# Output rows of a fused attention, MoE and MLP kernel: one transfer per sequence instead of one per block

## The chip, the cores and the metric

One core of a Trainium2 chip runs the whole kernel as one program. The metric is the device time of an execution in microseconds; a table below gives it for the kernel before. TensorE (PE in the profile) does the matrix products, VectorE (DVE) and ScalarE (ACT) the elementwise work, GpSimd (POOL) a few copies and the gathers, and SyncE (SP) does nothing but issue transfers. ScalarE can issue transfers too, on a queue of its own.

## The reference

Three stages, the output of one being the input of the next:

```python
attn_out = _attn_ref(q, k, v, i_gate, f_gate, o_gate)   # (2, 8, 768, 40), a recurrence over 768 steps
x = attn_out.transpose(0, 2, 1, 3).reshape(1536, 320)    # rows: sequence b = 0, then sequence b = 1
x = _moe_ref(x, w_gate, w_noise, noise, w1, w2)          # top 2 of 8 experts, 320 -> 1024 -> 320, relu
h = x @ w_in                                             # 320 -> 2048
g = h * np.clip(h + 3.0, 0.0, 6.0) / 6.0
return g @ w_out                                         # (1536, 320) float32
```

Rows 0 to 767 of the output belong to the first sequence, rows 768 to 1535 to the second.

## The kernel before

The 1536 rows are handled in 12 blocks of 128. Attention works on 64 time steps of both sequences at once, so a block k holds, in partitions 0 to 63, steps 64k to 64k+63 of sequence 0, and in partitions 64 to 127 the same steps of sequence 1. This layout stays through all three stages. The list `rows` (line 231) names the two halves of the partitions: `rows[0]` is 0 to 63 and `rows[1]` is 64 to 127.

The schedule is written out by hand. After the attention, a list of units is worked off in order: nine of the experts, then six of the last MLP. Each unit of the MLP holds four blocks, 512 rows in all, and one half `g` of the 2048 hidden features; three units do the first half, three the second. Of a unit, `L1` (a first product, an activation on ScalarE and VectorE that ends in a tile `hb`) and `L2` (the second product, accumulated in four PSUM banks `u.acc`, one for each block) alternate over eight slices of features. `hbs` holds the `hb` tiles whose `L2` is still to be issued, and `drain` issues them and calls `finish` at the last one of a unit.

`finish(u, tiles)` (line 893) takes the finished banks out. For an expert it copies them to a tile `yo` and sends that to the DRAM tensor `Yd` (line 919), with 128 rows or, for the last tile of a full expert, 64. For the first three MLP units it leaves a sixth of the sums in SBUF (`part`). For the last three, on which the change bears, VectorE adds bank and `part` into a `yo` tile of 128 x 320 fp32 (line 921; four buffers), and SyncE sends that tile to the output (line 923):

```python
outr = out.rearrange("(b k t) d -> k b t d", b=B, k=NT)          # line 889
V.scalar_tensor_tensor(y, u.acc[i][:, 0:DM], 1.0 / 6.0, part, OP.mult, OP.add)
nc.sync.dma_start(outr[k], y)                                    # line 923
```

`outr[k]` is a view of 2 x 64 x 320: two stretches of the output, each 64 rows of 1280 bytes that lie one behind another, and 768 rows apart. So there are 12 output transfers of 160 KB: four behind the unit before the last but one, four behind the last but one, and four at the very end. The last unit is cut differently from the others. With `v` and `w` the two last `hb` tiles, the kernel ends like this (lines 1226 to 1232):

```python
v, w = hbs
L2(*v, (0, 1, 2))
L2(*w, (0, 1))
finish(units[-1], (0, 1))
L2(*v, (3,))
L2(*w, (2, 3))
finish(units[-1], (2, 3))
```

Nothing is computed after the second `finish`; the program ends when its last transfer has landed. Line 1294 closes the program, and waits for all transfers are put down to it.

Of the kernel before, what the change touches and what calls it, by code (L numbers as in the profile page):

```python
# [23 lines left out]
B, H, S, D = 2, 8, 768, 40  # L24
# [44 lines left out]
def mlstm_moe_mlp(ctx, tc, qk, kv, on, gf, gf6, wg, nz, w1, w2, w_in, w_out, cf, cb, cs, ci, out):  # L69
    nc = tc.nc  # L70
    V, A, G, T = nc.vector, nc.scalar, nc.gpsimd, nc.tensor
# [159 lines left out]
    rows = [slice(0, 64), slice(64, 128)]  # L231
# [500 lines left out]
    def unit(e, tiles, nf=8):  # L732
        u = U()
        u.e, u.tiles, u.nf = e, tiles, nf
        u.N = sum(n for _, n in tiles)
        u.off, o = [], 0
        for _, n in tiles:
            u.off.append(o)
            o += n
        u.half = u.N - 64 if tiles[-1][1] == 64 else None  # L740
        u.bg = {}
        u.xo = 0
        u.st = e % 2
        u.l1 = [0, 1, 7]
        return u
# [4 lines left out]
    units = [unit(0, first), unit(1, first2), unit(1, rest2)]  # L750
# [138 lines left out]
    outr = out.rearrange("(b k t) d -> k b t d", b=B, k=NT)  # L889
# [3 lines left out]
    def finish(u, tiles=None):  # L893
        for i, (s, n) in enumerate(u.tiles):
            if tiles and i not in tiles:
                continue
            if u.e >= 8:
                if not parts:
                    parts.append(wp.tile([128, 5120], F32, name="SA1"))
                part = parts[0][:, s // 128 * DM:(s // 128 + 1) * DM]  # L900
            if u.e >= 8 and u.g == 0:

                if i % 2:
                    V.tensor_scalar(part, u.acc[i][:, 0:DM], 1.0 / 6.0, None, OP.mult)
                else:
                    A.mul(part, u.acc[i][:, 0:DM], 1.0 / 6.0)
                continue
            y = wp.tile([128, DM], F32, name="yo", bufs=4)
            if u.e < 8:
                if n == 64:  # L910
                    y2 = wp.tile([64, DM], F32, name="yo2", bufs=1)
                    A.copy(y2, u.acc[i][64:128, 0:DM])
                    V.tensor_tensor(y[0:64], u.acc[i][0:64, 0:DM], y2, OP.add)
                elif i % 2:
                    V.tensor_copy(y, u.acc[i][:, 0:DM])
                else:
                    A.copy(y, u.acc[i][:, 0:DM])
                r = OV + (7 - u.e) * CAP + s
                nc.sync.dma_start(Yd[r:r + n], y[0:n])
            else:  # L920
                V.scalar_tensor_tensor(y, u.acc[i][:, 0:DM], 1.0 / 6.0, part, OP.mult, OP.add)  # L921
                k = s // 128
                nc.sync.dma_start(outr[k], y)

    zy = []

# [195 lines left out]
    def drain(k):  # L1122
        while len(hbs) > k:
            v = hbs.pop(0)
            L2(*v)
            spot[0] += 1
            u, f, lo, hi = v[0:4]
            if f == u.nf - 1 and u.i == M0:
                finish(u, range(lo, hi))
            elif u.steps[-1] == v[1:4]:  # L1130
                finish(u)
# [95 lines left out]
# [5 lines that stand above are left out]
# [66 lines left out]
```

## Time and profile before

| what | us |
|---|---|
| three runs | 574.27, 573.12, 571.0 |
| their median | 573.12 |
| the profiled execution, its own time | 572.06 |
| its span, first to last instruction | 570.3 |
| outside the span in that execution | 1.76 |
| mean granted clock of TensorE, share of full | 0.913 |

The page of the profile gives each engine's busy time, then the span in 40 equal slices of 14.3 us: a digit is the busy share in tenths, and the lowest lines give the share of the 16 DMA engines that was busy and the bytes that they moved. Other views list a stretch's instructions in order of time, cut a stretch into windows, name the chain of work that ended last, and say who waited for whom. "SPq" and "ACTq" are the sequencers of SyncE and ScalarE, on which transfers are issued. A transfer's issue is one instruction there; the bytes move later and show only in the DMA columns.

### The profile page before, as it was taken

Reading aid. Unit: us, or ns where it says so; the run is one execution under the profiler, and the core shown is the slowest. Engines: PE = TensorE matmul, PEld = TensorE weight load, DVE = VectorE, ACT = ScalarE, POOL = GpSimd, SP = SyncE. Lnnn points to the kernel's source line nnn. Section 1 sums busy time; section 2 is a strip of 40 time slices with the busy share of each in tenths; the row PEclk is TensorE's granted clock in tenths of the full one; section 3 lists DMA queues with packets and bytes.
Section 4 is the critical chain, followed back from the end, with each engine's and each line's share of the span. In section 5 each row is a group of like instructions: output and inputs, shape, how many; then the busy total and the mean of one; then the engine's idle time right before and its main releaser. Section 6 shows DMA issues by size and latency. Waiting matters only on the chain. (4 is left out here: it accounts for less than half of the span.)

```text
span 570.3 us, 10786 instructions
## 1 busy us (share of the span) xinstructions
PE 511.8 (90%) x4154; PEld 454.1 (80%) x4159; DVE 345.5 (61%) x841; ACT 227.5 (40%) x469; POOL 130.8 (23%) x164
## 2 busy tenths in 40 slices
PE   4768897786799999999999999998999999999990
PEld 1446675565689999999999899988989999999980
DVE  5167856474576587878787877467696434343440
ACT  4142433213345453545444453354553333333320
POOL 4133253534731320201111002548300100000000
PEclk9795757677879999999999999999999999999996
DMA  7697879502548478788878769678633400010101
GB/s 233 160 245 229 212 92 95 101 30 63 136 121 270 166 259 281 277 278 280 265 280 282 246 236 297 191 226 278 165 112 115 139 1 0 1 35 12 35 16 43
DMA packets 46846, 92.74 MB, mean 163 GB/s; under 512 B 7128, under 2 KB 30520, under 8 KB 46792
## 3 DMA queue, kind: packets, MB, share of 16 engines
q1 hardware_dynamic: 38980, 69.29, 41.8%
q0 software_dynamic: 6464, 19.94, 11.6%
q10 hardware_dynamic: 1348, 2.79, 1.6%
q8 instruction: 33, 0.54, 0.4%
q14 instruction: 21, 0.17, 0.1%
HBM read 68.73 MB, written 23.07 MB: 161 GB/s over the span
## 5 line engine op out<-in xcount | busy, mean ns | idle before, releaser
L861 DVE SCALAR_TENSOR_TENSOR r<-r,bank 128x512 f32<-128x512 f32 (+1 forms) x56 | 34.2, 610 | 83.2 <-ACT r L860 81.5
L846 PE MATMUL bank<-XH,SB 128*128 128x448 f32 (+3 forms) x280 | 78.9, 352 | 0.5 <-PEq L944 0.3
L849 ACT ACTIVATE hb<-bank 128x448 fp32r<-128x448 f32 (+2 forms) x80 | 37.2, 468 | 96.8 <-PE bank L846 75.2
L860 ACT ACTIVATE r<-bank,cft 128x512 f32<-128x512 f32 (+1 forms) x56 | 35.0, 626 | 98.5 <-PE bank L846 88.8
L846 PE MATMUL bank<-XL,SB 128*128 128x448 f32 (+3 forms) x192 | 68.9, 359 | 0.0
L882 PE MATMUL bank<-SB,hb 128*128 128x320 f32 x192 | 62.0, 323 | 3.3 <-ACT hb L833 3.3
L773 POOL DMA_INDIRECT XG<-Xd,idx x32 | 32.4, 1011 | 134.6 <-PE bank L783 106.7
L882 PE MATMUL bank<-SA,hb 128*128 128x320 f32 x192 | 61.0, 318 | 0.9 <-issue 0.9
L883 PE MATMUL bank<-SA,hb 128*128 128x320 f32 x192 | 59.7, 311 | 0.3 <-issue 0.3
L884 PE MATMUL bank<-SA,hb 128*128 128x320 f32 x192 | 59.7, 311 | 0.1
L884 PE MATMUL bank<-SB,hb 128*128 128x320 f32 x192 | 59.7, 311 | 0.0
L883 PE MATMUL bank<-SB,hb 128*128 128x320 f32 x192 | 59.2, 309 | 0.0
L846 PEld LDWEIGHTS bank<-XH,SB 128*128 128x128 f32 x280 | 51.5, 193 | 5.8 <-issue 1.2
L846 PE MATMUL bank<-XH,SA 128*128 128x448 f32 (+2 forms) x200 | 53.1, 337 | 2.3 <-issue 2.3
L882 PEld LDWEIGHTS bank<-SB,hb 128*128 128x128 f32 x192 | 36.2, 188 | 5.0 <-ACT hb L833 3.9
L846 PE MATMUL bank<-XL,SA 128*128 128x448 f32 (+2 forms) x120 | 40.1, 335 | 0.0
L846 PEld LDWEIGHTS bank<-XL,SB 128*128 128x128 f32 x192 | 36.8, 192 | 3.0 <-DVE XL L785 0.2
L846 PEld LDWEIGHTS bank<-XH,SA 128*128 128x128 f32 x200 | 36.1, 193 | 3.7 <-issue 1.7
L242 PE MATMUL bank<-qk 128*64 128x128 f32 x192 | 23.1, 375 | 17.3 <-DMA qk<-in_qk_dram 11.3
L883 PEld LDWEIGHTS bank<-SA,hb 128*128 128x128 f32 x192 | 36.4, 189 | 2.2 <-issue 1.1
L882 PEld LDWEIGHTS bank<-SA,hb 128*128 128x128 f32 x192 | 36.4, 190 | 1.7 <-issue 0.5
L855 DVE SCALAR_TENSOR_TENSOR hb<-bank,hb 128x64 fp32r<-128x64 f32 x64 | 14.1, 221 | 38.5 <-ACT hb L849 37.1
(198 smaller groups left out, 1152.8 us busy)
## 6 DMA issues: line engine op xcount, KB each, us to landing
raw<-in_w_dram SPq DMA_DIRECT2D x18, 640.0 KB
raw<-in_w_dram SPq DMA_DIRECT2D x18, 512.0 KB
qk<-in_qk_dram SPq DMA_DIRECT2D x22, 240.0 KB
craw<-in_w_in_dram SPq DMA_DIRECT2D x8, 640.0 KB
craw<-in_w_out_dram SPq DMA_DIRECT2D x8, 640.0 KB
raw<-in_w_dram SPq DMA_DIRECT2D x18, 256.0 KB
Yd<-yo SPq DMA_DIRECT2D x24, 160.0 KB
kv<-in_kv_dram SPq DMA_DIRECT2D x11, 324.0 KB
```

What stands on the lines that cost most here:

```text
L242: T.matmul(s4[rows[b], 2 * p:2 * p + 2, :], q[:, p, 1, rows[b]], q[:, p, 0:4:3, rows[b]], start=True, stop=True)
L773: G.indirect_dma_start(out=XG[0:n, (u.xo + i) % 4, :], out_offset=None, in_=Xd[0:CUT[u.i] * 128] if early else Xd[:, :], in_offset=bass.In ...
L846: T.matmul(p, a, b, start=(i == 0), stop=(i == 7))
L849: A.activation(hb[:, 0:N], p, AF.Relu)
L855: V.scalar_tensor_tensor(hb[:, N:N + 64], p[:, o:N], 0.0, hb[:, o:N], OP.max, OP.subtract)
L860: A.activation(r, p, AF.Relu, bias=three)
L861: V.scalar_tensor_tensor(r, r, 6.0, p, OP.min, OP.mult)
L882: T.matmul(p, h, wh, start=s, stop=False)
L883: T.matmul(p, h, wl, start=False, stop=False)
L884: T.matmul(p, hb[:, lo:lo + 128], wh, start=False, stop=t)
```

## The change

Each output block is sent as two transfers of 64 rows, one for each sequence, from the two halves of the partitions. For the first eight blocks both go out on SyncE's queue. For the four blocks of the last unit the first sequence's half goes out on SyncE's queue, the second's on ScalarE's.

```diff
@@ -920,7 +920,9 @@
             else:
                 V.scalar_tensor_tensor(y, u.acc[i][:, 0:DM], 1.0 / 6.0, part, OP.mult, OP.add)
                 k = s // 128
-                nc.sync.dma_start(outr[k], y)
+
+                for b in range(B):
+                    (A if b and u is units[-1] else nc.sync).dma_start(outr[k, b], y[rows[b]])
```

## Rows read from the trace of the kernel before

**Rows 1.** The page: busy share, transfers and bytes in 40 slices.

```profile
span 570.3 us, 10786 instructions
PE 511.8 (90%) x4154; PEld 454.1 (80%) x4159; DVE 345.5 (61%) x841; ACT 227.5 (40%) x469; POOL 130.8 (23%) x164
PE   4768897786799999999999999998999999999990
DMA  7697879502548478788878769678633400010101
```

**Rows 2.** The chain of waits from 553.5 us: start, length, what; its end.

```profile
554.55 0.16 PE bank L884
554.71 0.02 issue
554.73 0.49 DVE yo L921
```

**Rows 3.** Windows over the end: engines' busy us, clock, DMA share, GB/s.

```profile
554.50:555.50 1.00, 0.19 (x2) 0.00 (x0) 0.72 (x2) 0.00 (x0) 0.00 (x0) 1.00 0.13 35
557.50:562.50 5.00, 0.00 (x0) 0.00 (x0) 0.00 (x0) 0.00 (x0) 0.00 (x0) 0.68 0.13 49
562.50:567.50 5.00, 0.00 (x0) 0.00 (x0) 0.00 (x0) 0.00 (x0) 0.00 (x0) 0.50 0.13 49
568.80:568.90 0.10, 0.00 (x0) 0.00 (x0) 0.00 (x0) 0.00 (x0) 0.00 (x0) 0.50 0.05 13
569.00:570.30 1.30, 0.00 (x0) 0.00 (x0) 0.00 (x0) 0.00 (x0) 0.00 (x0) 0.50 0.00 0
```

**Rows 4.** Waits of SyncE's sequencer after 552 us: total us, times, longest.

```profile
SPq L1294 <- DMA out_dram<-yo: 9.0, 3, 3.3
```

**Rows 5.** Transfers after 553 us: packets by size, and the issues.

```profile
DMA packets 521, 0.66 MB, mean 38 GB/s; under 512 B 8, under 2 KB 520, under 8 KB 520
out_dram<-yo SPq DMA_DIRECT2D x4, 160.0 KB
```

**Rows 6.** VectorE in order of time, 552.5 to 556 us, waits in brackets.

```profile
552.97 0.93 DVE L921 SCALAR_TENSOR_TENSOR yo<-bank,SA 128x320 f32<-128x320 f32 x2 [1.05 <-PE bank L884]
554.29 0.93 DVE L921 SCALAR_TENSOR_TENSOR yo<-bank,SA 128x320 f32<-128x320 f32 x2 [0.39 <-PE bank L884]
```

**Rows 7.** Line 923 on SyncE: first issue, third issue, then durations in ns.

```profile
553.49 0.51 SPq L923 DMA_DIRECT2D out_dram<-yo  x1
554.81 1.45 SPq L923 DMA_DIRECT2D out_dram<-yo  x1
...
L923 SPq DMA_DIRECT2D out_dram<-yo x12: 511/908/3523, 501.1 to 556.4; - x12
```

**Rows 8.** A 64-row transfer of line 919: issue, then windows of its bytes.

```profile
358.96 0.49 SPq L919 DMA_DIRECT2D Yd<-yo  x1
...
360.00:360.10 0.10, 0.10 (x2) 0.10 (x2) 0.00 (x0) 0.10 (x1) 0.00 (x0) 1.00 0.00 0
360.20:360.30 0.10, 0.10 (x3) 0.10 (x2) 0.09 (x1) 0.00 (x0) 0.00 (x0) 1.00 0.88 205
360.30:360.40 0.10, 0.10 (x2) 0.10 (x2) 0.10 (x1) 0.00 (x0) 0.00 (x0) 1.00 0.93 205
360.50:360.60 0.10, 0.10 (x3) 0.10 (x2) 0.10 (x1) 0.00 (x0) 0.00 (x0) 1.00 0.22 52
360.60:360.70 0.10, 0.10 (x3) 0.10 (x3) 0.03 (x1) 0.00 (x0) 0.00 (x0) 1.00 0.01 0
```

**Rows 9.** Both queues' issues at the start; then ScalarE's last instruction.

```profile
0.73 1.88 ACTq L101 DMA_DIRECT2D ont<-in_on_dram  x4
...
0.74 0.42 SPq L87 DMA_DIRECT2D gft<-in_gf_dram  x1
1.22 0.40 SPq L89 DMA_DIRECT2D cbt<-in_cb_dram  x1
...
550.58 0.62 ACT L833 CAST hb<-r 128x512 fp32r<-128x512 f32 x1 [0.24 <-DVE r L861]
```

**Rows 10.** The first four output blocks: a window, and line 921's waits.

```profile
505.00:510.00 5.00, 5.00 (x30) 4.55 (x29) 1.29 (x2) 1.75 (x3) 0.00 (x0) 1.00 0.13 49
...
DVE yo L921 <- PE bank L884: 1.4, 2, 1.1
```

## The prediction

> **What bounds the kernel now.** I read the page first. TensorE is busy for 90% of the span and at nine tenths or more in nearly every slice of the second half, so this is a kernel bound by matrix products, but its last slice shows a 0 [rows 1]. The reader should stop there: a slice is 14.3 us long, and in that one the busiest engine does nothing while the DMA line still shows a 1. Next I read the chain of waits at its end. It runs along TensorE's second product and stops with VectorE's addition into `yo`, which starts at 554.73 us and takes 0.49 [rows 2]. The span is 570.3 us [rows 1], so 15.1 us lie behind the end of the chain, which follows instructions and not the bytes of a transfer.
>
> The windows show what fills them. From 554.5 us on the DMA engines move 35 and then a steady 49 GB/s, at a busy share of 0.13 of 16 engines; the last bytes move in the window from 568.8 to 568.9, and after that nothing moves until the end of the span [rows 3]. 0.13 of 16 is 2.1: two engines carry all of it. The stretch holds four transfers of 160 KB, 0.66 MB in 512 packets of 1280 bytes and 8 small ones [rows 5]. SyncE's closing waits say the same in another way: it waits three times for these transfers, 9.0 us in all, 3.3 at the longest [rows 4]. So the four blocks land one behind another, some 3.3 us apart. That is 128 rows on two engines: at 49 GB/s for both, one engine moves 1280 bytes in 1280/24.5 = 52 ns, and 64 x 52 ns = 3.34 us. The view of the output that is sent has an outermost count of two (the sequences), each a stretch of 64 rows; two engines with 64 packets each fits that.
>
> **The change part by part.** *Four blocks at the end, two transfers of 64 rows each.* The trace has no 64-row output transfer, but it has one of the very same shape: an expert's last tile goes to `Yd` as 64 rows of 1280 bytes from 64 partitions to consecutive rows. The one at 358.96 us ran when nothing else moved: issued for 0.49 us, no bytes up to 360.1, then 0.88 and 0.93 of the 16 engines busy at 205 GB/s, and done at 360.6 [rows 8]. So that transfer is spread over about all 16 engines and its last byte moves 1.64 us after its issue began. There are eight such transfers in the trace; this is the one with a quiet surrounding. I take it for the price of a half block, since it differs from the halves in the change only in the tensor written and, for every second one, in the partitions read (64 to 127).
>
> *When the last one is issued.* The additions of the four blocks come in pairs, 552.97 to 553.90 and 554.29 to 555.22 [rows 6], and their times don't hang on the transfers, since the four `yo` buffers were free: line 921 waited for TensorE alone [rows 10]. The first issue now starts at 553.49, right behind the first addition [rows 7], so it stays. On SyncE four issues of 64 rows remain. The third block's starts at 554.81 as now [rows 7]; at 0.49 us [rows 8] it ends at 555.30. Between two issues of SyncE lie 0.06 us at the start of the kernel (0.74 + 0.42 to 1.22) [rows 9]; with a wait to pass I estimate 0.1. So the fourth starts at 555.4, a little after its data are there at 555.22. In the old kernel the third issue took 1.45 and others up to 3.52 us [rows 7]; I read this as the issue being held up behind transfers that don't drain, which goes away with them, and nobody waits for it either way except the next issue.
>
> *ScalarE's queue.* Its four issues run beside SyncE's. ScalarE's last instruction of work ends at 551.2 us [rows 9], so nothing is queued behind the waits for VectorE that the new issues bring: the cover is complete, and were there still an activation to come it would have waited till 555.2. Whether two queues can issue side by side the start of the kernel shows: four issues on ScalarE fill 0.73 to 2.61 us while SyncE issues at 0.74 and 1.22 for 0.42 and 0.40 us each [rows 9]. At 0.47 us per issue the fourth half of ScalarE starts at 555.25 to 555.4 too. Both last transfers together are 160 KB; beside each other on 16 engines at the 205 GB/s of one or more they can delay each other by at most the 0.5 us that one moves bytes [rows 8], which goes into the range.
>
> *The end.* From the last byte (568.9) to the end of the span lie 1.4 us without a byte [rows 3]: landing, SyncE's last waits, the close. I keep them. SyncE's other closing waits, which now fall into the shadow of the transfers, then run from 555.9 on, while the last half is under way, so they cost nothing.
>
> *Eight earlier blocks.* Their transfers ran at the same 0.13 and 49 GB/s, but with TensorE busy 5.00 of 5.00 us beside them [rows 10], and no one waits for them. Eight more issues on SyncE, 4 us, lie in stretches where it waits for VectorE. Nothing gained, nothing lost. Two transfers that read one tile may give VectorE one more wait per `yo` buffer in the last unit; below 0.1 us, by the 0.02 us "issue" piece of the chain [rows 2].
>
> *The sum.* 555.4 + 1.64 + 1.4 = 558.45 us of span, against 570.3: 11.8 us less. On the profiled execution's own time that is 572.06 - 11.8 = 560.3 us. That execution lies 1.06 us below the median of the runs (573.12), from which it would be 561.3. All four known executions have a mean of 572.6, and I take 572.6 - 11.8 = 560.8 us.
>
> *Bounds.* Most favourable: both last halves are issued the moment VectorE is done, 555.22, and the issue costs as little as the 0.40 us of the row at 1.22 [rows 9]: 555.22 + 1.55 + 1.4 = 558.2, 12.1 less. Least favourable with the spread intact: the eight issues go one by one, 0.6 us apart, as if there were one queue. Then the last starts at 553.49 + 7 x 0.6 = 557.7 and the span is 560.7, 9.6 less; spreading over eight engines instead of 16 (512 packets / 8 x 52 ns = 3.3 us from 554.6 on, end at 559.4) lies between. Against the runs shown: 571.0 - 12.1 = 558.9 and 574.27 - 9.6 = 564.7.
>
> [...]
>
> **The rivals.** *No gain.* The halves go one after another at the present pace, two engines for each: 8 x 32 x 52 ns = 13.3 us, as now, and 572.6 us. For it speaks that block transfers to this very tensor have never run faster than 49 GB/s in the trace [rows 3, 10]; against it the 64-row transfer at 205 GB/s with the same inner stretch [rows 8]. Chance 4%. [...]
>
> *Slower.* Today each sequence's stretch of 64 rows sits on one engine. If the spread were made by that stretch, so that a transfer of one stretch goes whole to one engine, and to the same one each time, all eight halves would queue there: 512 x 52 ns = 26.6 us instead of 13.3, so 572.6 + 13.3 = 585.9 us. It decides by the number of engines of a half: with two it is a draw, with one the change loses, with more it wins. Rows 8 speak against it, as a single engine can't be 0.93 of 16. Chance 3%.
>
> *Issue-bound.* The spread works but issuing on the two queues goes in file, or the first transfer on ScalarE's queue after more than 540 us starts late; 9.6 us gained, 563.0 us. The rows at the start speak against it [rows 9], but no row shows ScalarE issuing late in the kernel. Chance 9%.
>
> **How the numbers follow.** Forecast 84%, issue-bound 9%, no gain 4%, slower 3%. The first two lie in 558.9 to 564.7, so the range is that; leaving out the other two costs under 1 in 10. A measurement of this kernel can tell about 0.5%, 2.9 us, from no change; both cases of a gain are far beyond it. Faster 0.93, same 0.04, slower 0.03.
>
> **What would show it.** In the profile after: the windows behind the last addition show a DMA share well above 0.13, in peaks toward 0.9, and GB/s in the hundreds; the last byte moves near 557.0 us; SyncE's closing wait for the output shrinks from three waits and 9.0 us to about one of 1.5; line 923 has 20 issues on SyncE and 4 on ScalarE of about 0.5 us, none over 1; the span is near 558.5, its part up to 555.2 as before. A share that stays at 0.13 or falls to 0.06 would show the prediction wrong (no gain, slower), and a last issue past 556 us would point to the issue-bound case.

## The result, and the profile after

| | before | after |
|---|---|---|
| median, us | 572.67 (4 runs) | 557.51 (4 runs) |
| lowest to highest, us | 571.0 to 574.27 | 556.19 to 567.38 |
| profiled execution: time, span, us | 572.06, 570.3 | 556.19, 554.4 |
| ratio after/before, 95% interval | | 0.9728 [0.9681, 0.9775] |

One of the four executions after, at 567.38 us, ran in a slower state (mean granted clock of TensorE 0.899, where the other three have 0.916 to 0.932), and the ratio leaves it out.

The kernel became faster by 15.2 us in the medians, 15.9 in the two profiled executions. Forecast were 11.8 us and 560.8 us, with a range from 558.9 to 564.7. The sign was right; the median after lies 1.4 us below the range.

The page after, three of its lines; the last slice (now 13.9 us) has TensorE at 6 tenths instead of 0 [rows 1].

```profile
span 554.4 us, 10807 instructions
PE   3777786897949999999999999989999999999996
DMA  7697867512447678888888768885921610001011
```

Windows over the end after (engines' busy us, clock, DMA share, GB/s), which answer to [rows 3]:

```profile
549.50:550.50 1.00, 0.49 (x4) 0.22 (x2) 0.92 (x2) 0.00 (x0) 0.00 (x0) 1.00 0.54 143
550.50:551.50 1.00, 0.00 (x0) 0.00 (x0) 0.02 (x1) 0.00 (x0) 0.00 (x0) 1.00 0.90 245
551.50:552.50 1.00, 0.00 (x0) 0.00 (x0) 0.00 (x0) 0.00 (x0) 0.00 (x0) 1.00 0.89 249
552.70:552.80 0.10, 0.00 (x0) 0.00 (x0) 0.00 (x0) 0.00 (x0) 0.00 (x0) 1.00 0.01 0
552.80:554.40 1.60, 0.00 (x0) 0.00 (x0) 0.00 (x0) 0.00 (x0) 0.00 (x0) 0.98 0.00 0
```

The share rises from 0.13 to 0.90, the rate from 49 to 249 GB/s, and the bytes are gone within some 3 us. The packets of this stretch tell the same:

```profile
DMA packets 641, 0.66 MB, mean 104 GB/s; under 512 B 128, under 2 KB 640, under 8 KB 640
```

Beside the 512 packets of 1280 bytes there are 128 small ones, 16 for each of the eight halves; before there were 8, two for each of the four blocks [rows 5]. So two small packets a transfer went with a share of 0.13, which is 2.1 of the 16 engines, and 16 with 0.90, which is 14.4. VectorE's last additions, SyncE's closing wait for the output, and the last issue on each queue, after:

```profile
549.59 0.93 DVE L921 SCALAR_TENSOR_TENSOR yo<-bank,SA 128x320 f32<-128x320 f32 x2 [0.39 <-PE bank L884]
...
SPq L1296 <- DMA out_dram<-yo: 1.5, 2, 0.8
...
550.66 0.55 SPq L925 DMA_DIRECT2D out_dram<-yo  x1
...
550.93 0.58 ACTq L925 DMA_DIRECT2D out_dram<-yo  x1
```

The 9.0 us of waiting in [rows 4] are 1.5. The important reading is a subtraction. The last addition ends at 549.59 + 0.93 = 550.52 us, so 3.9 us of span lie behind it; before, it ended at 555.22 [rows 6], with 15.0 behind it (worked out from times to the hundredth). I call that stretch the tail and the rest the body. Of the 15.9 us by which the two profiled executions differ the tail lost 11.2; the expectations below say 11.1, from the rounded 15.0 and 3.9. The other 4.7 us lie ahead of the last addition, in the body. Where in the body, the first transfer to `Yd` (line 919) tells: its first and last start are the two numbers behind the durations. Before:

```profile
L919 SPq DMA_DIRECT2D Yd<-yo x32: 332/493/1523, 164.7 to 372.9; - x32
```

After:

```profile
L919 SPq DMA_DIRECT2D Yd<-yo x32: 332/498/1442, 159.9 to 368.9; - x32
```

The lead is 4.8 us at the first of these transfers, and from there to the last addition both kernels take the same (390.5 and 390.6 us). It arose before 160 us, where no changed line has run. So there were two theories to tell apart. A: the change is worth the 11.2 us of the tail, and the rest is chance. B: the change, by its early issues or by its place in the program, also makes the body some 4 us faster.

### The profile page after: what moved, and what is told of

Same layout as the page of the kernel before. It is cut to its first block, busy times and chain, and to the rows that moved or that the text cites. A ratio compares the mean times of both kernels' runs of the same rounds, so it can differ in the third digit from the quotient of the medians.

```text
span 554.4 us, 10807 instructions
## 1 busy us (share of the span) xinstructions
PE 505.8 (91%) x4159; PEld 449.5 (81%) x4159; DVE 345.7 (62%) x841; ACT 228.1 (41%) x469; POOL 132.5 (24%) x164
## 5 line engine op out<-in xcount | busy, mean ns | idle before, releaser
L882 PE MATMUL bank<-SB,hb 128*128 128x320 f32 x192 | 62.7, 326 | 2.2 <-ACT hb L833 1.7
L773 POOL DMA_INDIRECT XG<-Xd,idx x32 | 31.2, 974 | 131.2 <-PE bank L783 106.1
L884 PE MATMUL bank<-SB,hb 128*128 128x320 f32 x192 | 60.3, 314 | 0.0
L883 PE MATMUL bank<-SB,hb 128*128 128x320 f32 x192 | 59.8, 312 | 0.0
L882 PEld LDWEIGHTS bank<-SB,hb 128*128 128x128 f32 x192 | 36.7, 191 | 4.0 <-ACT hb L833 1.9
L883 PEld LDWEIGHTS bank<-SB,hb 128*128 128x128 f32 x192 | 36.8, 192 | 0.8
L884 PEld LDWEIGHTS bank<-SB,hb 128*128 128x128 f32 x192 | 36.6, 191 | 0.5 <-DVE hb L834 0.2
```

The costliest lines, as they stand in the source:

```text
L773: G.indirect_dma_start(out=XG[0:n, (u.xo + i) % 4, :], out_offset=None, in_=Xd[0:CUT[u.i] * 128] if early else Xd[:, :], in_offset=bass.In ...
L882: T.matmul(p, h, wh, start=s, stop=False)
L883: T.matmul(p, h, wl, start=False, stop=False)
L884: T.matmul(p, hb[:, lo:lo + 128], wh, start=False, stop=t)
```

## Experiments

**The change again**, unaltered, beside the kernel before.

> The changed kernel once more. Theory A (only the end changes; the rest of the 15 us was chance of the first rounds): from the last addition to the end of the span 3.9 us instead of 15.0, so 11.1 us less, a ratio near 0.980 to the kernel before, and in its profile the last addition ends somewhere between 550 and 557 us as it falls out. Theory B (the change also shortens the part ahead of the first output transfer by 4 us): a ratio near 0.973 again, and the first output transfer near 496 us as in the first profile after, not near 501.

Ratio 0.9851 [0.9786, 0.9916], medians 562.14 (6 runs) and 573.3 (17 runs). The profiled execution's last addition ended at 551.34 us, its tail is 3.9 us. The interval holds theory A's 0.980 and leaves out B's 0.973. In the 17 runs the kernel before lay between 566.48 and 580.55 us: a width of 14 us, where the first runs had shown 3.3.

**The change a third time**, in another comparison.

> The changed kernel against the kernel before a third time. Theory A (the end alone, 11.1 us, and chance): ratio near 0.980 with tail 3.9 us; the time itself lies wherever the chip's own time before lies, less 11 us. Theory B (a further 4 us ahead of the end): 0.973.

Ratio 0.979 [0.9719, 0.9861], medians 562.48 (6 runs) and 571.98 (11 runs); last addition at 557.19, tail 4.0 us. This is the same program as in the result, with a body 6.7 us longer. Its interval alone would still hold B's 0.973 at its edge; together with the one before, A is the better account.

**Only the first eight blocks in halves.**

```diff
+                if u is units[-1]:
+                    nc.sync.dma_start(outr[k], y)
+                else:
+                    for b in range(B):
+                        nc.sync.dma_start(outr[k, b], y[rows[b]])
```

> Only the first eight blocks go out in halves; the last four stay whole, on SyncE's queue. Theory A: nobody waits for these eight, ratio 1.000, tail behind the last addition 15.0 us. Theory B, if the gain ahead of the end comes from these issues or from their place in the program: 4 us less, ratio near 0.993.

Ratio 0.9984 [0.9931, 1.0036], medians 571.46 (12 runs) and 573.3 (17 runs). Additions and closing waits in its trace:

```profile
546.25 0.93 DVE L921 SCALAR_TENSOR_TENSOR yo<-bank,SA 128x320 f32<-128x320 f32 x2 [0.39 <-PE bank L884]
...
SPq L1298 <- DMA out_dram<-yo: 9.0, 3, 3.3
```

The tail is back at 15.2 us (span 562.4, last addition 547.19), with the same three waits as in [rows 4]. The early halves give at most 0.7%, and nothing that can be told from zero. Its body is 8 us shorter than that of [rows 6], so a short body comes without the new tail too.

**Only the last four blocks in halves.**

```diff
+                if u is units[-1]:
+                    for b in range(B):
+                        (A if b else nc.sync).dma_start(outr[k, b], y[rows[b]])
+                else:
+                    nc.sync.dma_start(outr[k], y)
```

> Only the last four blocks go out in halves, on the two queues; the first eight stay whole. Theory A: the full gain of the end, 11 us, ratio near 0.980, equal to the change run beside it. Theory B: 4 us less gain than the change run beside it, if the early blocks bring them.

Ratio 0.9813 [0.9737, 0.9889], against 0.9851 for the change beside it; tail 3.9 us, last addition at 556.53. The whole new tail comes from the last four blocks.

**All halves on SyncE's queue.**

```diff
-                    (A if b and u is units[-1] else nc.sync).dma_start(outr[k, b], y[rows[b]])
+                    nc.sync.dma_start(outr[k, b], y[rows[b]])
```

> All halves on SyncE's queue. The spread over the engines stays, the second queue goes. If the issue sets the end: eight issues of about 0.55 us in file from the first addition on, the last starting some 3.9 us after the first instead of 2.1, so 1.7 to 1.9 us longer than the change run beside it (ratio near 0.983 if that one is at 0.980). If the bytes or the landing set it: no difference. If the second queue were the source of the gain: back to 1.000.

Ratio 0.981 [0.9735, 0.9885]. By the ratio alone it can't be told from the change. The tail can: its last two issues on SyncE, and the eight issues' durations in ns,

```profile
560.49 1.19 SPq L924 DMA_DIRECT2D out_dram<-yo  x2
...
L924 SPq DMA_DIRECT2D out_dram<-yo x8: 466/587/738, 556.5 to 561.1; - x8
```

The eighth issue starts at 561.1, 2.8 us behind the last addition (558.28) where the change's last starts 0.41 behind. The tail is 6.2 us, 2.3 longer than the change's; expected were 1.7 to 1.9. So splitting the blocks takes the tail from 15.0 to 6.2 us, 8.8 less, and the second queue, which saves issue time, takes off another 2.3. This is one trace, of an execution of 566.5 us; that its length doesn't make the tail is seen from the change's third time, where a body nearly as long (557.2) has a tail of 4.0.

**Whole blocks, every second one of the last four on ScalarE's queue.**

```diff
-                nc.sync.dma_start(outr[k], y)
+                (A if k % 2 and u is units[-1] else nc.sync).dma_start(outr[k], y)
```

> Whole blocks as before, but of the last four every second one goes out on ScalarE's queue. If the number of DMA engines of a transfer sets its time and both queues put a two-part transfer on the same two engines: 512 packets on two engines as before, tail behind the last addition 15.0 us, DMA share 0.13. If each queue had engines of its own: two blocks behind one another on each, 6.7 us of bytes instead of 13.3, tail near 8.5 us, share 0.25.

One run beside the kernel before (559.61 against a median of 561.68); what decides is the trace:

```profile
543.50:550.00 6.50, 0.00 (x0) 0.00 (x0) 0.00 (x0) 0.00 (x0) 0.00 (x0) 0.62 0.13 46
550.00:556.00 6.00, 0.00 (x0) 0.00 (x0) 0.00 (x0) 0.00 (x0) 0.00 (x0) 0.50 0.13 49
```

Still 0.13 of the engines and 49 GB/s, tail 15.2 us. The second queue brought no engines: whole blocks from both queues fall on the same two, else the share would be 0.25. Alone, the queue takes nothing off the tail.

**Quarters and two engines.** Two kernels with the same number of transfers, bytes and issues, of which one cuts a half into 32 and 32 rows (below), the other into 62 and 2, with the pairs (0, 62) and (62, 64).

```diff
+                    for lo, hi in ((0, 32), (32, 64)):
+                        (A if b and u is units[-1] else nc.sync).dma_start(
+                            outr[k, b, lo:hi], y[64 * b + lo:64 * b + hi])
```

> Each half goes out as two transfers of 32 rows on the half's queue: 16 transfers at the end instead of 8. If a 32-row transfer also uses 16 engines, the issues set the end: eight per queue at 0.55 to 0.6 us, the last some 2.4 us behind the last addition instead of 0.4, tail near 5.9 us. If a transfer cost its 1.8 us of start-up in file, 8 x 1.8 us per queue: tail near 15.

> Each half goes out as 62 rows and 2 rows, on the half's queue: as many transfers, issues and bytes as in quarters. If the outermost count of a transfer decides on how many engines it runs (62 divides by 2 but by no other number up to 16), 62 rows lie 31 each on two engines: 8 x 32 x 52 ns = 13.3 us of bytes, tail near 15 us, DMA share 0.13 and the time back at that of the kernel before. If the gain came from having two stretches in two transfers, or from the second queue: as quarters, near 5.9 us.

Windows of the quarters, and the packets of their end:

```profile
540.80:541.80 1.00, 0.00 (x0) 0.00 (x0) 0.21 (x1) 0.00 (x0) 0.00 (x0) 1.00 0.62 182
541.80:542.80 1.00, 0.00 (x0) 0.00 (x0) 0.00 (x0) 0.00 (x0) 0.00 (x0) 1.00 0.60 178
...
DMA packets 769, 0.66 MB, mean 94 GB/s; under 512 B 256, under 2 KB 768, under 8 KB 768
```

Windows of 62 and 2 rows, and their packets:

```profile
550.00:556.00 6.00, 0.00 (x0) 0.00 (x0) 0.00 (x0) 0.00 (x0) 0.00 (x0) 0.50 0.13 49
556.00:557.50 1.50, 0.00 (x0) 0.00 (x0) 0.00 (x0) 0.00 (x0) 0.00 (x0) 0.50 0.13 50
...
DMA packets 545, 0.66 MB, mean 39 GB/s; under 512 B 32, under 2 KB 544, under 8 KB 544
```

One execution of each was measured, 547.92 us for the quarters and 562.04 for 62 and 2 rows, beside a median of 561.68 for the kernel before; the traces decide. Quarters: tail 5.1 us (expected 5.9; a 32-row issue took 0.40 us instead of 0.55 to 0.6). With 62 and 2 rows on the same two queues the share is 0.13, the rate 49 GB/s, and the tail 15.7 us: the old kernel's end, though each transfer is one stretch of output rows. Its 32 small packets are two for each of the 16 transfers; the quarters have 256, 16 for each. This is the run that shows the cause. What decides is neither the number of transfers nor the second queue nor the single stretch, but on how many engines a transfer's rows are spread. The traces show it for four outermost counts: 2 x 64 rows and 62 rows at a share of 0.13 with two small packets a transfer, 64 rows at 0.90 and 32 rows at 0.60 to 0.62 with 16. The divisor that the expectation counts with fits these four; that it holds for others was not shown.

**The kernel before against itself**, beside the last three kernels.

> The kernel before against itself. Ratio 1.000 with the width that the comparison has from chance alone; tail 15.0 us; the last addition ends anywhere between 547 and 559 us, by the clock granted in the first 160 us.

Ratio 0.9985 [0.995, 1.002], medians 560.05 (12 runs) and 561.68 (17 runs). So in this comparison the kernel before runs at 561.7 us, in the others at 573.3 and 572.0; the comparisons with 561.7 and 572.0 ran on the same chip. Tail 15.1, last addition at 541.17: the body is 14 us shorter than in the profiled execution before, with not a line changed. One difference is the granted clock of TensorE (the column behind the engines; a share of full speed: the traces before and after record 0.5 and 1.0 alone, and a window shows their mean) in the stretch where the attention ends. In the kernel before, as first profiled:

```profile
100.00:150.00 50.00, 40.52 (x544) 32.53 (x547) 30.06 (x137) 14.17 (x47) 24.63 (x39) 0.74 0.36 75
```

In this execution of it:

```profile
100.00:150.00 50.00, 38.84 (x553) 32.43 (x552) 35.16 (x159) 19.92 (x58) 28.66 (x45) 0.93 0.30 83
```

**Block 1's halves on GpSimd's queue**, an attempt to shorten the tail further.

```diff
+                    e = nc.sync
+                    if u is units[-1]:
+                        e = G if i == 1 else (nc.sync, A)[b]
+                    e.dma_start(outr[k, b], y[rows[b]])
```

> As the change, but the two halves of the last unit's second block go out on GpSimd's queue, so that SyncE and ScalarE have three issues each at the end instead of four. If the issue of the last halves is held up by the ones before, ScalarE's last one starts 0.15 us behind the last addition instead of 0.41 and the tail is 3.6 us instead of 3.9. If GpSimd's path is slower to start or to close, the tail is 3.9 or longer.

The step it was made for worked: ScalarE's last issue started 0.20 us behind the last addition. But the tail grew to 9.3 us (562.58 us in the one execution, beside a median of 571.98). A window of its tail, SyncE's closing wait and GpSimd's closing instruction, a drain:

```profile
553.60:560.50 6.90, 0.00 (x0) 0.00 (x0) 0.00 (x0) 0.00 (x0) 0.00 (x0) 0.67 0.00 0
...
SPq L1298 <- PEq L1298: 5.9, 2, 5.4
...
L1298 POOLq DRAIN  x1: 9065/9065/9065, 550.6 to 550.6; - x1
```

The same instruction in the change:

```profile
L1296 POOLq DRAIN  x1: 10824/10824/10824, 439.1 to 439.1; - x1
```

6.9 us pass without a byte after the last one, where the change has 1.7. The view names TensorE's sequencer in the program's close, which had nothing new to do. The trace shows another: GpSimd's drain starts at 550.6, beside its last issue, takes 9.07 us, and ends at 559.7; SyncE has passed its own waits by 554.5, and its next instruction comes at 559.8. In the change the drain is as long, 10.8 us, but it starts at 439.1, at the end of GpSimd's other work, and nobody waits for it. So the two transfers cost this time by moving the start of the drain to the end of the program. It is one run, and what sets the drain's length was not tried.

All executions with a trace, in one table, made from each one's span, its last addition (start plus duration) and the mean granted clock in its window from 0 to 170 us:

| kernel | last addition ends, us | tail, us | mean clock to 170 us |
|---|---|---|---|
| before | 555.2 | 15.0 | 0.74 |
| early blocks only | 547.2 | 15.2 | 0.79 |
| before, second time | 541.2 | 15.1 | 0.82 |
| queue only | 542.6 | 15.2 | 0.81 |
| 62 and 2 rows | 544.6 | 15.7 | 0.75 |
| after | 550.5 | 3.9 | 0.79 |
| change again | 551.3 | 3.9 | 0.76 |
| change, third time | 557.2 | 4.0 | 0.75 |
| last blocks only | 556.5 | 3.9 | 0.74 |
| one queue | 558.3 | 6.2 | 0.74 |
| quarters | 541.0 | 5.1 | 0.85 |
| third queue | 551.2 | 9.3 | 0.76 |

The tail is a property of the kernel and repeats within 0.2 us. The body spreads over 17 us and shows no relation to the change: the same program after has 550.5, 551.3 and 557.2, the one before 555.2 and 541.2. Most of the spread arises early, where all these programs are the same: the first transfer to `Yd` starts between 148.0 and 164.8 us, and from there to the last addition the traces take 389.6 to 395.4. The granted clock differs there too, and not later: from 200 to 540 us it is 0.99 to 1.00 in all twelve.

## Why the prediction was right and where it failed

*What bounds the end* held: the last product and addition, then bytes on two engines (0.13). The 62-row run, which rebuilds the two engines out of single stretches (0.13 again), gives the tail back, 15.7 us.

*The price of a half block* held roughly. The last half was issued on ScalarE at 550.93, and the bytes end at about 552.7, 1.8 us later instead of the 1.64 of [rows 8].

*When the last one is issued*: 0.14 us behind the last addition on SyncE, as forecast (0.2). On ScalarE it was 0.41: its issues took 0.55 to 0.72 us, not the 0.47 taken from [rows 9], and the fourth stood behind the third. That is 0.2 us more. That line 921 waits for TensorE alone holds for all 12 blocks: the second line of [rows 10] is of 495 to 571 us.

*The end*: the close after the last byte took 1.7 us, not 1.4. The step said that SyncE's other closing waits cost nothing; but they come in the order of the program, and behind the wait for the half that landed last SyncE had six more and a drain to pass:

```profile
L1296 SPq EVENT_SEMAPHORE  x6: 28/28/28, 553.1 to 553.4; - x6
L1296 SPq DRAIN  x1: 13/13/13, 553.5 to 553.5; - x1
```

The seven start 0.06 us apart and take 0.43 us in all; before, one wait and a drain stood there, so 0.3 us are new. With these three the tail is 3.9 us instead of the 3.2 forecast, and the gain of the end 11.2 us instead of 11.8.

*Eight earlier blocks* held: no gain, no loss that can be told from zero. The detail that no issue would last over 1 us did not: SyncE's longest of the 20 took 1.88 us, among the early blocks, with nobody waiting.

*The step that failed* is the one that turned the gain into a time and a range, "Against the runs shown: 571.0 - 12.1 = 558.9 and 574.27 - 9.6 = 564.7". It took the spread of three runs, 3.3 us, for the spread of the kernel, and so put the chance difference of two bodies at nothing beyond it ("its part up to 555.2 as before"). Seventeen runs of the kernel before spread over 14 us, the lower eleven of them over 8.2, and a comparison of its own had a median 11 us lower. The body of the profiled execution after ended at 550.5 instead of 555.2, 4.7 us earlier; 0.6 of the forecast gain were lost in the tail, and 560.3 + 0.6 - 4.7 = 556.2 us is the time of that execution. A range worked from the tail and the width of the body, some 7 us to each side, would have held the result. Too small as well are the 0.5% that a measurement was said to tell: the same change came out at 0.9728, 0.9851 and 0.979.

So theory A is the better account. The first ratio, 0.9728, overstates the change; two repeats gave 0.9851 and 0.979, and 11.2 us off 572.67 would be 0.980. Inside each comparison the body is the shorter, the higher the granted clock of the first 170 us (0.85, 0.82, 0.81, 0.75 with 541.0, 541.2, 542.6, 544.6 in one of them); between comparisons it is not (0.75 also goes with 557.2), and no run changed that clock by itself. So it is a correlation, and what sets the body's length stays open. That the first comparison's runs after fell on the short side by chance is argued from these widths, and not shown.

*The rivals.* No gain is refuted for 64 rows and realised by the kernel with 62. Slower did not come about, the share being 0.90; that a sequence's stretch of 64 rows sits on one engine was an estimate from the 0.13 and the 3.3 us of a block. Issue-bound was seen with one queue, at a cost of 2.3 us.

## What to carry to other kernels

Look at the DMA share of a stretch that no engine covers: here a share that stayed at 0.13, two sixteenths, went with transfers of 2 x 64 and of 62 rows, and their outermost count was the place to look. The transfer was worth cutting to 64 rows (0.90) or 32 (0.60 to 0.62); for other counts, try the cut and read the share. A second queue took 2.3 us of issue time off the tail of the halves, and nothing off that of whole blocks (15.2 us). And judge a gain at the end of a program by the tail in the trace, which repeats within 0.2 us, when whole executions differ by 14.

## What the hardware showed that was not expected

- The same program's time before the last addition varied from 541.2 to 555.2 us between two profiled executions, and its median from 561.68 to 573.3 us between comparisons.
- Whole blocks sent from SyncE and from ScalarE share the same two DMA engines (share 0.13, 49 GB/s, tail 15.2 us).
- With two transfers on GpSimd's queue near the end, its closing drain of 9.07 us began only at 550.6 instead of 439.1 us, and 6.9 us passed between the last byte and the end of the span, against 1.7 without.
- A transfer had two small packets where the share was 0.13 (2 x 64 rows, 62 rows), and 16 where it was 0.90 (64 rows) or 0.60 to 0.62 (32 rows).
